# A decode block's output projection: wo in one transfer, all 32 heads projected at once, and more unread matmuls around it

## The chip, the cores and the metric

The kernel runs on one NeuronCore of a Trainium2 chip. The core has a matrix engine (TensorE, PE in the profile; its weight loads are shown apart, as PEld), a vector engine (VectorE, DVE), an activation engine (ScalarE, ACT), GpSimd (POOL) and SyncE (SP), which here only issues DMA transfers. Each engine works through its own list of instructions in order, and they meet through semaphores. The metric is the device time in microseconds (us) of one execution.

## The reference

One token passes a pre-norm transformer block: attention over a cached context, and a gated feed-forward part. Everything is bf16, and the caches are most of the bytes: 32 heads, 4096 positions, 128 values per position, for K and for V.

```python
def _A_ref(x, k_cache, v_cache, wq, wo):          # x [1,1,640]; caches [1,32,4096,128]
    q = (x @ wq).reshape(B, Sq, Hq, Dh).transpose(0, 2, 1, 3)
    scores = einsum("bhqd,bhkd->bhqk", q, k) * Dh ** -0.5
    o = einsum("bhqk,bhkd->bhqd", softmax(scores), v)
    return o.transpose(0, 2, 1, 3).reshape(B, Sq, Hq * Dh) @ wo      # wo [4096, 640]
def _B_ref(x, w_gate, w_up, w_down):              # Df = 1728
    return (gelu(x @ w_gate) * (x @ w_up)) @ w_down
h  = x + _A_ref(layernorm(x), k_cache, v_cache, wq, wo)
h2 = h + _B_ref(layernorm(h), w_gate, w_up, w_down)
```

## The kernel before, in words

**Storage and transfers.** Three large SBUF buffers ("slots") take turns. SyncE issues all the big transfers on one queue, in this order: wq, K0, V0, K1, V1, K2, K3, V2, V3, wo, w_gate, w_up, w_down, where K0 to K3 and V0 to V3 are the caches of eight heads each. A transfer waits until its slot has been read to the end: the third V tile's last reader (`done[("V", 2)]`) frees the slot into which wo goes, and the fourth K tile's last reader frees the one for w_gate. wo comes as two transfers of 2560 KB, one for the rows of heads 0 to 15 and one for those of heads 16 to 31. In each, partition p gets 16 consecutive rows of wo.

**The four groups.** `NG` is 4, and group G has eight heads. For each of eight chunks of a K tile, `score_mult` multiplies K by q on VectorE (L310), eight matmuls against an identity fold the products on TensorE (L318 where the weights are loaded, L30 where they are used again), and `score_sum` reduces them on VectorE (L327). Then `softmax` takes the maximum and the exponentials (L332 to L337) and spreads the weights over a block layout (L341). `attend` multiplies them with V: 64 matmuls (L353). `pick` takes out of their result what belongs to each head (L359, L362, L363), and `head_sum` adds up the partial sums over partitions on TensorE, the softmax denominators with `hb` (L367) and the weighted values with `hs` (L369).

**The pairs of groups.** Two groups make a half of 16 heads, called t. `normalize(t)` divides by the denominators (L373, L374), `spread(t)` copies the 16 rows over all partitions with a matmul against the mask `sel` (L377), and `take(t)` keeps on each partition the values that belong to its rows of wo (L381 with the mask `m8`, then L386, which gives `aP`). `proj_part(t, lo, hi)` then projects: for each i in the range and for each half of wo's 640 columns one matmul of 320 columns, four at a time in different column strips of the array (L398 for the first half of the columns; L30, through `matmul_again`, for the second). The 64 matmuls of both t accumulate in two PSUM banks.

**The order around the change.** It is written out by hand. In the third group (G = 2), while VectorE and TensorE work on the scores, normalize, spread and take of the first half are put between the chunks (after chunks 4, 5 and 6). After the last attend TensorE's list has: eight i of the first half, one unread matmul, the last head sum, four more i, the spread of the second half, the last four i, four unread matmuls, and the 16 i of the second half.

**The unread matmuls.** `run_on(n)` puts n matmuls of 512 columns on TensorE that multiply an identity by itself, into a PSUM bank that nobody reads afterwards. They wait for no other engine. The first is L453 and the others go through `matmul_again`, so that they show as L30 with the names bank<-id_b.

**After the projection.** The sums are copied out of the two banks as a bf16 part and a rest (L469, L470, L471), turned to columns (L477), added to x (L486) and normalized (L487). The gate and up matmuls (L510) wait for w_gate and w_up, the down matmuls (L552, L561) for three parts of w_down, and two copies (L564) lead to the output transfer.

Of the kernel before, what the change touches and what calls it, by code (L numbers as in the profile page):

```python
# [5 lines left out]
FP32 = mybir.dt.float32  # L6
BF16 = mybir.dt.bfloat16
ALU = mybir.AluOpType
ACTF = mybir.ActivationFunctionType
AX = mybir.AxisListType  # L10

D = 640
H = 32
DH = 128
# [6 lines left out]
NG = 4  # L21
# [90 lines left out]
def bass_sequential_preLN__gqa_block_cached__glu_gated_geglu__decode_kernel(nc, A_x, A_k_cache, A_v_cache, A_wq, A_wo, B_x, B_w_gate, B_w_up, B_w_down, out):  # L112
    sb = lambda name, shape, dt: nc.alloc_sbuf_tensor(name, shape, dt)
# [15 lines left out]
    hlnT = sb("hlnT", [128, 5], BF16)  # L129
    rz = sb("rz", [16, 2], FP32)  # L130
    po_r = sb("po_r", [128, 2, DH + 1], FP32)
    m4 = sb("m4", [128, 4], FP32)
    hs = sb("hs", [128, 24], FP32)
    hb = sb("hb", [128, 24], FP32)
    hbx = sb("hbx", [128, 8, 4], BF16)
    aT = sb("aT", [16, 2, 128], BF16)
    aP = sb("aP", [128, 2, 16], BF16)
    sel = sb("sel", [16, 16, 8], BF16)
    m8 = sb("m8", [128, 8], FP32)
    aM = sb("aM", [128, 8, 16], FP32)  # L140
    sel4 = sb("sel4", [128, 4], BF16)
# [20 lines left out]
    class Cut:  # L162
# [3 lines left out]
        def take(self, n, parts=128):  # L166
            ap = self.slot[0:parts, self.at:self.at + n]
            self.at += n
            return ap
    first_t = Cut(slots[2], 5 * 4096)  # L170
    ones_b = first_t.take(128)
    m4_t = first_t.take(128).rearrange("p (a b) -> p a b", a=4)
    hs_t = first_t.take(128).rearrange("p (a b c) -> p a b c", a=8, b=4)
    m8_t = first_t.take(128).rearrange("p (a b) -> p a b", a=8)
    par_t = first_t.take(128).rearrange("p (a b) -> p a b", a=2)
# [18 lines left out]
    wq_sb = slots[2][:, 0:5 * 4096]  # L194
    wo_sb = slots[0][:, 0:32 * D].rearrange("p (t i n) -> p t i n", t=2, i=16)
    wg_sb = slots[2][:, 0:5 * DF].rearrange("p (c n) -> p c n", c=5)
# [39 lines left out]
    def mask(dst, src, pattern, base, cm, op, *deps):  # L236
        return GP(lambda e: e.affine_select(dst, src, pattern=pattern, compare_op=op, fill=0.0, base=base,
                                            channel_multiplier=cm), *deps)
    c_idb = mask(id_b[:, :], ones_b[:, 0:128], [[1, 128]], 0, -1, ALU.is_equal, c_onesb)
    c_hz = GP(lambda e: e.memset(hs[:, :], 0.0))  # L240
    c_bz = GP(lambda e: e.memset(hb[:, :], 0.0))
    c_hb = mask(hb[:, 8:16], ones_b[:, 0:8], [[-16, 8]], 0, 1, ALU.is_ge, c_bz)
    c_hb = mask(hb[:, 8:16], hb[:, 8:16], [[16, 8]], 15, -1, ALU.is_ge, c_hb)
    c_m4 = mask(m4_t, ones_b[:, 0:128].rearrange("p (a b) -> p a b", a=4), [[-1, 4], [-4, 32]], 0, 1, ALU.is_equal)
# [5 lines left out]
    c_hx = mask(hbx[:, :, :], hbx[:, :, :], [[16, 8], [0, 4]], 15, -1, ALU.is_ge, c_hx)  # L250
    c_sel = mask(sel[:, :, :], ones_b[0:16, 0:128].rearrange("p (a b) -> p a b", a=16), [[1, 16], [0, 8]], 0, -1, ALU.is_equal)
    c_m8 = mask(m8_t, ones_b[:, 0:128].rearrange("p (a b) -> p a b", a=8), [[-1, 8], [-8, 16]], 0, 1, ALU.is_equal)

    c_odd = V(lambda e: e.reduce_sum(odd[:, :], hb[:, 8:16].rearrange("p (a b) -> p b a", b=2), axis=AX.X), c_hb)
    c_far = V(lambda e: e.tensor_scalar(far[:, :, :], odd[:, :].unsqueeze(2).to_broadcast([128, 2, 16]), -1e38, 1e38, ALU.mult, ALU.add), c_odd)
    c_m4 = V(lambda e: e.reduce_sum(m4[:, :], m4_t, axis=AX.X), c_m4)
    c_m8 = V(lambda e: e.reduce_sum(m8[:, :], m8_t, axis=AX.X), c_m8)
    c_hs = V(lambda e: e.reduce_sum(hs[:, 8:16], hs_t.rearrange("p a b c -> p a (b c)"), axis=AX.X), c_hs, c_hz)
    c_o4 = V(lambda e: e.reduce_max(ones4[:, :], sel4[:, :], axis=AX.X), c_s4)
# [37 lines left out]
    q1 = V(lambda e: e.tensor_copy(qb[:, :, :].rearrange("p g d -> p (g d)"), ps_q[:, :]), qd)  # L297
    free2 = [qd, c_par, c_m4, c_m8, c_hs, c_idb]

    folds, reds, exps, pbs, pvs, mks, evs, hds, nbs = {}, {}, {}, {}, {}, {}, {}, {}, {}  # L300
    z4s, spr, aPs = {}, {}, {}
    held = [False]

    def other(fn, *d):
        held[0] = False
        return T(fn, *d)
# [58 lines left out]
    def head_sum(G):  # L365
        g, at = G % 2, 132 * (G // 2)
        other(lambda e: e.matmul(ps_a[0:16, at + DH:at + DH + 1], hb[:, 8 - 8 * g:24 - 8 * g], po_r[:, g, DH:DH + 1],  # L367
                                 start=(g == 0), stop=(g == 1), skip_group_check=True), exps[G], z4s.get(G // 2 - 1), c_hb)
        hds[G] = T(lambda e: e.matmul(ps_a[0:16, at:at + DH], hs[:, 8 - 8 * g:24 - 8 * g], po_r[:, g, 0:DH],  # L369
                                      start=False, stop=(g == 1), skip_group_check=True), evs[G], c_hs)  # L370

    def normalize(t):
        rc = V(lambda e: e.reciprocal(rz[:, t:t + 1], ps_a[0:16, 132 * t + DH:132 * t + DH + 1]), hds[2 * t + 1])  # L373
        z4s[t] = V(lambda e: e.tensor_scalar(aT[:, t, :], ps_a[0:16, 132 * t:132 * t + DH], rz[:, t:t + 1], None, ALU.mult), rc)  # L374

    def spread(t):
        spr[t] = other(lambda e: e.matmul(ps_z[:, 32:160], sel[:, :, :].rearrange("p a b -> p (a b)"), aT[:, t, :], start=True, stop=True),  # L377
                       z4s[t], c_sel)

    def take(t):  # L380
        m = V(lambda e: e.tensor_tensor(out=aM[:, :, :], in0=ps_z[:, 32:160].rearrange("p (q i) -> p q i", q=8),  # L381
                                        in1=m8[:, :].unsqueeze(2).to_broadcast([128, 8, 16]), op=ALU.mult), spr[t], c_m8)

        def fn(e):
            with nc.allow_low_precision(reason="one of the eight terms is not zero"):
                return e.reduce_sum(aP[:, t, :], aM[:, :, :].rearrange("p q i -> p i q"), axis=AX.X)  # L386
        aPs[t] = V(fn, m)

    def proj_part(t, lo, hi, *ws):
        def fn(e):  # L390
            for i4 in range(lo, hi, 4):
                for half in range(2):
                    for i in range(i4, i4 + 4):
                        a = 32 * (i - i4)
                        args = (bank[half][a:a + 1, 0:320], aP[:, t, i:i + 1], wo_sb[:, t, i, 320 * half:320 * half + 320])
                        start, stop = t == 0 and i < 4, t == 1 and i >= 12
                        if half == 0:
                            r = e.matmul(*args, start=start, stop=stop)  # L398
                        else:
                            r = matmul_again(nc, *args, start, stop, (128, 32), (0, a))  # L400
            return r
        return T(fn, *ws)

    PARTS = 4
    for G in range(NG):
        for c in range(8):
            if c == 5 and G == 3:
                attend(2)
            score_mult(G, c)
            if c >= 1:  # L410
                score_sum(G, c - 1)
            if c == 1 and G in (1, 2):
                pick(G - 1)
            if c == 3 and G in (1, 2):
                head_sum(G - 1)
            if c == 4 and G == 2:
                normalize(0)
            if c == 5 and G == 2:
                spread(0)
            if c == 6 and G == 2:  # L420
                take(0)
            if c == 7 and G == 3:
                pick(2)
        score_sum(G, 7)
        softmax(G)
        if G == 0:
            load("K", 1, *free2)
            load("V", 1, done[("K", 0)])
        if G == 3:
            head_sum(2)  # L430
        if G != 2:
            attend(G)
        if G == 0:
            load("K", 2, done[("V", 0)])
        if G == 1:
            load("K", 3, done[("K", 1)])
            load("V", 2, done[("V", 1)])
        if G == 2:
            load("V", 3, done[("K", 2)])


    d_wo = [P.dma("sync", wo_sb[:, t, :, :], A_wo[2048 * t:2048 * t + 2048, :].rearrange("(p i) n -> p i n", i=16), done[("V", 2)])
            for t in range(2)]
    free = done[("K", 3)]
# [13 lines left out]
    pick(NG - 1)  # L458
    proj_part(0, 0, 8, aPs[0], d_wo[0], reds[(NG - 1, 7)])
    run_on(1)  # L460
    head_sum(NG - 1)
    normalize(1)
    proj_part(0, 8, 12)
    spread(1)
    take(1)
    proj_part(0, 12, 16)
    run_on(4)
    pr = proj_part(1, 0, 16, aPs[1], d_wo[1])
    hi = [V(lambda e: e.tensor_copy(A_hi[0:97, 0:320], bank[0][0:97, 0:320]), pr),  # L469
# [4 lines left out]
    def columns(part, start):  # L474
# [5 lines left out]
        return fn  # L480
    run_on(1)
    T(columns(A_hi, True), *hi, c_o4)
    run_on(1)
    pr = T(columns(A_lo, False), *lo)
    run_on(1)
    h = V(lambda e: e.tensor_add(hT[:, 0:5], xx[:, 0:5], ps_p[:, 0:5]), pr)  # L486
# [110 lines left out]
```

## Time and profile before

| | |
|---|---|
| time, median of three runs | 201.8 us (201.78 to 201.81) |
| time of the profiled execution | 202.04 us |
| its span, first to last instruction | 200.8 us |
| TensorE, VectorE, ScalarE busy | 112.5, 117.7, 6.5 us |
| bytes read | 84.23 MB, 420 GB/s over the span |
| TensorE's granted clock, mean | 0.907 of full |

The profile is that of one execution. "Busy" times of TensorE are modelled from starts and lengths of pipelined matmuls, so that eight matmuls in a row that each take 0.39 us can follow each other at a much smaller distance. The chain of the profile is the work that ended last, followed back from the last instruction: at each step to what released it, or to the instruction before it on the same engine. In a line such as `L30 x3` the number behind x is the count of instructions, and an arrow `out<-in` names what is written and read. The granted clock is the share of TensorE's full clock that the hardware granted in a stretch.

### The profile page before, as it was taken

To read this page: it belongs to the slowest core of one execution; us is meant where nothing else is said; L and a number is where in the kernel's file an instruction comes from. 1 tells how busy PE (TensorE), PEld (TensorE's weight loads), DVE (VectorE), ACT (ScalarE), POOL (GpSimd) and SP (SyncE) were. 2 spreads that over 40 slices of the span, in tenths; PEclk is the share of its full clock that TensorE was granted. 3 is DMA by queue.
4 is the path that set the end of the run, shared out by engine and by line. 5 is a ranking of instruction groups with operands and counts; after the bars stand their busy time and mean duration, and the time that the engine had idled before them with its cause. 6 is when DMAs were issued, how large, how long until landed. Compare 5 with 4: busy or idle time off the path is not lost.

```text
span 200.8 us, 1539 instructions
## 1 busy us (share of the span) xinstructions
PE 112.5 (56%) x795; PEld 18.2 (9%) x501; DVE 117.7 (59%) x157; ACT 6.5 (3%) x17; POOL 3.5 (2%) x18
## 2 busy tenths in 40 slices
PE   0108000586675808476655095866167697497896
PEld 0103000000001200000021000000000030132423
DVE  3300100889975027999740469898789987814340
ACT  2100000000001000000010000000100000100111
POOL 7000000000000000000000000000000000000000
PEclk9999999999996666999979757899859999879999
DMA  9999999999999999999999999999999999999992
GB/s 343 433 465 431 418 418 418 418 418 496 496 431 444 397 431 418 431 431 418 418 418 421 470 483 444 431 418 431 418 431 431 418 418 388 432 416 435 434 396 97
DMA packets 2316, 84.32 MB, mean 420 GB/s; under 512 B 259, under 2 KB 390, under 8 KB 518
## 3 DMA queue, kind: packets, MB, share of 16 engines
q1 hardware_dynamic: 2308, 84.23, 97.6%
q8 instruction: 5, 0.08, 0.2%
q14 instruction: 1, 0.01, 0.0%
q10 hardware_dynamic: 2, 0.00, 0.0%
HBM read 84.23 MB, written 0.00 MB: 420 GB/s over the span
## 4 chain that ended last, share of the span: by engine, by line
DMA 39%; DVE 33%; PE 25%; ACT 1%; issue 1%; SPq 0%
DMA slot<-in_A_k_cache_dram 39%; DVE slot L310 20%; PE bank L30 11%; PE bank L353 8%; DVE sc L327 6%; PE bank L510 2%; DVE mix L341 1%; PE bank L552 1%; DVE mix L359 1%; PE bank L318 1%; ACT p_t L337 1%; DVE mix L362 1%; DVE mx L332 1%; PE bank L398 0%; DVE slot L471 0%
## 5 line engine op out<-in xcount | busy, mean ns | idle before, releaser
L310 DVE TENSOR_TENSOR slot<-slot,qb 128x4096 bf16<-128x4096 bf16 x32 | 72.7, 2283 | 33.5 <-DMA slot<-in_A_k_cache_dram 33.5
L30 PE MATMUL bank<-slot,id_b 128*128 128x512 bf16 x249 | 66.1, 418 | 27.4 <-DVE slot L310 27.4
L327 DVE TENSOR_REDUCE sc<-bank 128x32 f32<-128x512 f32 x32 | 22.0, 686 | 12.1 <-PE bank L30 12.1
L353 PE MATMUL bank<-slot,mix 128*32 128x512 bf16 x256 | 20.7, 495 | 8.8 <-DVE mix L341 8.8
L318 PE MATMUL bank<-slot,id_b 128*128 128x512 bf16 x7 | 3.4, 484 | 33.5 <-DVE slot L310 33.5
L353 PEld LDWEIGHTS bank<-slot,mix 128*32 128x32 bf16 x256 | 8.0, 120 | 77.6 <-DVE mix L341 42.4
L293 PE MATMUL bank<-slot,xlnM 128*32 128x512 bf16 x40 | 4.5, 630 | 7.2 <-DMA slot<-in_A_wq_dram 7.2
L341 DVE TENSOR_TENSOR mix<-p_t,hbx 128x512 bf16<-128x512 bf16 x16 | 5.7, 420 | 2.7 <-ACT p_t L337 2.7
L337 ACT ACTIVATE p_t<-sc,nb 128x256 bf16<-128x256 f32 x4 | 2.0, 507 | 162.2 <-DVE nb L336 162.2
L297 DVE CAST qb<-bank 128x512 bf16<-128x512 f32 x1 | 0.7, 692 | 10.2 <-PE bank L293 10.2
L359 DVE TENSOR_TENSOR mix<-bank,m 128x512 f32<-128x512 f32 x4 | 2.7, 684 | 4.3 <-PE bank L353 4.3
L266 PE MATMUL bank<-one_bf,x_keep 1*128 1x1 bf16 x5 | 0.4, 177 | 7.0 <-DMA x_keep<-in_A_x_dram 7.0
L453 PE MATMUL bank<-id_b 128*128 128x512 bf16 x11 | 4.2, 384 | 0.0
L318 PEld LDWEIGHTS bank<-slot,id_b 128*128 128x128 bf16 x7 | 0.7, 100 | 36.5 <-DVE slot L310 36.1
L30 PE MATMUL bank<-id_b 128*128 128x512 bf16 x13 | 3.8, 378 | 0.0
L510 PE MATMUL bank<-slot,hlnT 128*1 128x512 bf16 (+1 forms) x40 | 3.6, 478 | 0.1
L367 PEld LDWEIGHTS bank<-po_r,hb 128*16 128x16 f32 x8 | 0.4, 94 | 32.0 <-issue 32.0
L30 PE MATMUL bank<-slot,aP 128*1 128x320 bf16 x32 | 2.5, 298 | 0.0
L398 PE MATMUL bank<-slot,aP 128*1 128x320 bf16 x32 | 2.5, 298 | 0.0
L293 PEld LDWEIGHTS bank<-slot,xlnM 128*32 128x32 bf16 x40 | 1.6, 140 | 9.2 <-issue 9.2
L552 PE MATMUL bank<-slot,hm 128*2 128x160 bf16 x52 | 2.0, 232 | 0.0
L369 PE MATMUL bank<-po_r,hs 128*16 128x128 f32 x8 | 1.5, 274 | 0.6 <-DVE po_r L363 0.6
(94 smaller groups left out, 41.1 us busy)
## 6 DMA issues: line engine op xcount, KB each, us to landing
slot<-in_A_wq_dram SPq DMA_DIRECT2D x1, 5120.0 KB, 15.5
slot<-in_A_wo_dram SPq DMA_DIRECT2D x2, 2560.0 KB, 15.1
slot<-in_B_w_gate_dram SPq DMA_DIRECT2D x1, 2160.0 KB, 16.8
slot<-in_B_w_up_dram SPq DMA_DIRECT2D x1, 2160.0 KB, 21.5
slot<-in_B_w_down_dram SPq DMA_DIRECT2D x1, 1280.0 KB, 24.1
slot<-in_B_w_down_dram SPq DMA_DIRECT2D x1, 640.0 KB, 25.2
slot<-in_B_w_down_dram SPq DMA_DIRECT2D x1, 240.0 KB, 25.3
slot<-in_A_k_cache_dram SPq DMA_DIRECT2D x4, 39.0
```

Of the source, the lines that this page charges most:

```text
L30: return e.add_instruction(mybir.InstMatmult(name=nc.get_next_instruction_name(), engine=e.engine, start_tensor_calc=start, stop_tensor_ca ...
L293: i = e.matmul(ps_q[32 * j:32 * j + 32, :], xlnM[:, 160 * s + 32 * c:160 * s + 32 * c + 32], wq_j[:, c, 2 * j + s, :, :], start=(c == 0 an ...
L310: m = V(lambda e: e.tensor_tensor(out=kt, in0=kt, in1=qb[:, G, :].unsqueeze(1).to_broadcast([128, 32, DH]), op=ALU.mult), landed[("K", G)] ...
L318: i = e.matmul(*args, start=True, stop=False)
L327: reds[(G, c)] = V(lambda e: e.reduce_sum(sc[:, 32 * c:32 * c + 32], ps_f[c % 2][:, :].rearrange("p (g d) -> p g d", d=16), axis=AX.X), fo ...
L337: exps[G] = A(lambda e: e.activation(p_t[:, :], sc[:, :], ACTF.Exp, bias=nb[:, G:G + 1], scale=INV_SQRT_DH, accum_out=po_r[:, G % 2, DH:DH ...
L341: pbs[(G, n)] = pbs[G] = V(lambda e, lo=lo, hi=hi: e.tensor_tensor(out=p_bd[:, lo:hi, :].rearrange("p c (a r) -> p c a r", a=8), in0=p_t[: ...
L353: i = e.matmul(po[a:a + 32, 0:512], p_bd[:, c, :], vt[:, 4 * c:4 * c + 4, :], start=(c < 4), stop=(c >= 60))
L359: mks[G] = V(lambda e: e.tensor_tensor(out=po_m, in0=po[:, 0:512].rearrange("p (b d) -> p b d", b=4), in1=m4[:, :].unsqueeze(2).to_broadca ...
L453: i = e.matmul(*args, start=True, stop=True)
L510: i = e.matmul(po[32 * a:32 * a + 1, 512 * k:512 * k + 128 * n], hlnT[:, c:c + 1], cols, start=(c == 0), stop=(c == 4))
L552: i = e.matmul(ps_d[32 * t:32 * t + 2, :], hm[:, at:at + 2], wd_sb[:, PIECE * c + 160 * t:PIECE * c + 160 * t + 160], start=False, stop=(c ...
```

## The change

wo comes in one transfer of 5120 KB, in which partition p gets 32 consecutive rows. The four groups' head sums go to 32 partitions of one PSUM region, and normalize, spread and take are done once, for all 32 heads, after the last head sum; they leave the third group. Correspondingly `rz`, `aT`, `aP`, `sel` and `aM` are laid out for 32 heads, the mask `m8` with eight columns is gone and `m4` with four takes its place in `take`, and `hs` and `hb` grow from 24 to 56 columns. The projection is one block of 64 matmuls behind `take`.

The unread matmuls are set anew: three between the last attend and the last head sum, one between normalize and spread, twelve between take and the projection, then 2, 3 and 2 where there were 1, 1 and 1 in the steps behind the projection. Counted out of the diff, there are 16 up to the projection's end where there were 5, and 7 behind it where there were 3.

```diff
-    rz = sb("rz", [16, 2], FP32)
+    rz = sb("rz", [32, 1], FP32)
...
-    aT = sb("aT", [16, 2, 128], BF16)
-    aP = sb("aP", [128, 2, 16], BF16)
-    sel = sb("sel", [16, 16, 8], BF16)
-    m8 = sb("m8", [128, 8], FP32)
-    aM = sb("aM", [128, 8, 16], FP32)
+    aT = sb("aT", [32, 128], BF16)
+    aP = sb("aP", [128, 32], BF16)
+    sel = sb("sel", [32, 32, 4], BF16)
+    aM = sb("aM", [128, 4, 32], FP32)
...
-    wo_sb = slots[0][:, 0:32 * D].rearrange("p (t i n) -> p t i n", t=2, i=16)
+    wo_sb = slots[0][:, 0:32 * D].rearrange("p (i n) -> p i n", i=32)
...
     def head_sum(G):
-        g, at = G % 2, 132 * (G // 2)
-        other(lambda e: e.matmul(ps_a[0:16, at + DH:at + DH + 1], hb[:, 8 - 8 * g:24 - 8 * g], po_r[:, g, DH:DH + 1],
-                                 start=(g == 0), stop=(g == 1), skip_group_check=True), exps[G], z4s.get(G // 2 - 1), c_hb)
-        hds[G] = T(lambda e: e.matmul(ps_a[0:16, at:at + DH], hs[:, 8 - 8 * g:24 - 8 * g], po_r[:, g, 0:DH],
-                                      start=False, stop=(g == 1), skip_group_check=True), evs[G], c_hs)
...
+        lo = 24 - 8 * G
+        other(lambda e: e.matmul(ps_a[0:32, DH:DH + 1], hb[:, lo:lo + 32], po_r[:, G % 2, DH:DH + 1],
+                                 start=(G == 0), stop=(G == 3), skip_group_check=True), exps[G], c_hb)
+        hds[G] = T(lambda e: e.matmul(ps_a[0:32, 0:DH], hs[:, lo:lo + 32], po_r[:, G % 2, 0:DH],
+                                      start=False, stop=(G == 3), skip_group_check=True), evs[G], c_hs)
+
+    def normalize():
+        rc = V(lambda e: e.reciprocal(rz[:, :], ps_a[0:32, DH:DH + 1]), hds[3])
+        return V(lambda e: e.tensor_scalar(aT[:, :], ps_a[0:32, 0:DH], rz[:, 0:1], None, ALU.mult), rc)
+
+    def spread(z):
+        return T(lambda e: e.matmul(ps_z[:, 32:160], sel[:, :, :].rearrange("p a b -> p (a b)"), aT[:, :], start=True, stop=True), z, c_sel)
+
+    def take(sp):
+        m = V(lambda e: e.tensor_tensor(out=aM[:, :, :], in0=ps_z[:, 32:160].rearrange("p (q i) -> p q i", q=4),
+                                        in1=m4[:, :].unsqueeze(2).to_broadcast([128, 4, 32]), op=ALU.mult), sp, c_m4)
...
+                return e.reduce_sum(aP[:, :], aM[:, :, :].rearrange("p q i -> p i q"), axis=AX.X)
+        return V(fn, m)
+
+    def proj(e):
+        for i4 in range(0, 32, 4):
+            for half in range(2):
+                for i in range(i4, i4 + 4):
+                    a = 32 * (i - i4)
+                    args = (bank[half][a:a + 1, 0:320], aP[:, i:i + 1], wo_sb[:, i, 320 * half:320 * half + 320])
+                    if half == 0:
+                        r = e.matmul(*args, start=(i < 4), stop=(i >= 28))
+                    else:
+                        r = matmul_again(nc, *args, i < 4, i >= 28, (128, 32), (0, a))
+        return r
...
-            if c == 4 and G == 2:
-                normalize(0)
-            if c == 5 and G == 2:
-                spread(0)
-            if c == 6 and G == 2:
-                take(0)
...
-    d_wo = [P.dma("sync", wo_sb[:, t, :, :], A_wo[2048 * t:2048 * t + 2048, :].rearrange("(p i) n -> p i n", i=16), done[("V", 2)])
-            for t in range(2)]
+    d_wo = P.dma("sync", slots[0][:, 0:32 * D], A_wo[:, :].rearrange("(p i) n -> p (i n)", i=32), done[("V", 2)])
...
     pick(NG - 1)
-    proj_part(0, 0, 8, aPs[0], d_wo[0], reds[(NG - 1, 7)])
+    run_on(3)
+    head_sum(NG - 1)
+    z = normalize()
     run_on(1)
-    head_sum(NG - 1)
-    normalize(1)
-    proj_part(0, 8, 12)
-    spread(1)
-    take(1)
-    proj_part(0, 12, 16)
-    run_on(4)
-    pr = proj_part(1, 0, 16, aPs[1], d_wo[1])
+    sp = spread(z)
+    pw = take(sp)
+    run_on(12)
+    pr = T(proj, pw, d_wo, reds[(NG - 1, 7)])
...
-    run_on(1)
+    run_on(2)
     T(columns(A_hi, True), *hi, c_o4)
-    run_on(1)
+    run_on(3)
     pr = T(columns(A_lo, False), *lo)
-    run_on(1)
+    run_on(2)
```

## The prediction, made before the result was known

> **What bounds the kernel now.** I read the page's chain by line first, then the chain in order of time from 172 us on, then the timeline around the edited lines, the landings of wo, the waits of the last loads, and the windows with the granted clock. The page says that transfers and VectorE hold the chain:
>
> ```profile
> span 200.8 us, 1539 instructions
> DMA 39%; DVE 33%; PE 25%; ACT 1%; issue 1%; SPq 0%
> ```
>
> The transfer part ends at 113.06 us, when the third K tile lands. From there to the end the chain has compute only. Its end, in order of time (start, length, what):
>
> ```profile
> 174.69 5.22 PE bank L353 x63
> 179.94 0.70 DVE mix L359
> 182.10 0.35 DVE aT L374
> 182.50 0.23 PE bank L377
> 183.09 0.32 PE bank L453
> 183.41 0.65 PE bank L30 x3
> 184.06 0.24 PE bank L398 x4
> 185.29 0.50 DVE slot L469
> 192.64 1.08 PE bank L30 x5
> 193.72 1.76 PE bank L510 x14
> ```
>
> The reader is to see that TensorE runs in program order through L377 (spread), four unread matmuls (L453 and L30) and the second half of the projection, and that L30 x5, unread matmuls again, run right up to the up-projection at 193.72. So there is no free time between the projection and the end: what delays L469 delays the last copy.
>
> The first half of the heads: part of the work that the change removes, in the timeline:
>
> ```profile
> 129.72 0.68 DVE L327 TENSOR_REDUCE sc<-bank 128x32 f32<-128x512 f32 x1
> 130.33 0.14 DVE L373 RECIPROCAL rz<-bank 16x1 f32<-16x1 f32 x1
> 130.51 0.34 DVE L374 TENSOR_SCALAR aT<-bank,rz 16x128 bf16<-16x128 f32 x1
> 130.77 2.27 DVE L310 TENSOR_TENSOR slot<-slot,qb 128x4096 bf16<-128x4096 bf16 x1
> 132.97 0.67 DVE L327 TENSOR_REDUCE sc<-bank 128x32 f32<-128x512 f32 x1
> ```
>
> And the windows (start:end and length; busy time with instructions of PE, PEld, DVE, ACT, POOL; then the granted clock, the DMA share and GB/s):
>
> ```profile
> 167.65:171.06 3.41, 2.16 (x11) 0.00 (x0) 3.38 (x4) 0.00 (x0) 0.00 (x0) 1.00 0.80 339
> 171.06:174.48 3.42, 1.04 (x7) 0.22 (x4) 2.58 (x8) 0.60 (x2) 0.00 (x0) 1.00 0.98 419
> 174.48:177.89 3.41, 3.19 (x32) 1.25 (x36) 1.17 (x4) 0.00 (x0) 0.00 (x0) 0.50 1.00 426
> 177.89:181.30 3.41, 2.99 (x55) 1.11 (x39) 1.29 (x3) 0.00 (x0) 0.00 (x0) 1.00 0.99 422
> 181.30:184.72 3.42, 2.89 (x47) 0.80 (x28) 1.28 (x5) 0.00 (x0) 0.00 (x0) 1.00 0.99 423
> ```
>
> A window in which TensorE was busy for 1.04 of 3.42 us is followed by one at half clock; one with 2.16 is not. In the same view 119.86:123.28, with 1.36 busy, is also followed by half clock. From 177.89 to the last matmul the clock is full.
>
> **The change part by part.** The profiled execution took 202.04 us, its span 200.8 and 1.24 around it; the median of the three runs, 201.8, is 0.24 less. The sum is made on the trace and its difference put on the median. All shifts below are against the trace's own times.
>
> *Removed from VectorE in the third group (L373, L374, L381, L386 for the first 16 heads).* From the start of L327 to that of the next L310 normally takes 0.60 us (132.97 to 133.57). With normalize it takes 1.05 (129.72 to 130.77), with take 1.19 (135.77 to 136.96). So 0.45 + 0.59 = 1.04 us go. VectorE is the bound there: TensorE's folds of 1.89 us wait for L310 each time. Every later idle of VectorE up to 174 us is a wait for a TensorE fold that itself follows L310, so it moves along. The transfers needed are early: the last V tile is issued at 141.21 and takes 29.9 us to land, at 171.1, and the matmuls that read it start at 174.69. Bounds: nothing gained (a rival below), and 1.12, the sum of the four busy times; I take 1.04, the difference of starts. The removed L377 of that stage (0.23) sat in TensorE's idle time and is worth nothing.
>
> *Through the last attend (L353).* It starts at 173.65 instead of 174.69. The window 171.06 to 174.48 then holds 0.83 us of it and some 0.1 of the head sum, less than the 1.04 before, so 174.48 to 177.89 stays at half clock. At full clock its 64 matmuls take 3.57 us by the earlier one at 161.34, 0.054 each; at half clock 0.107. That is 15 matmuls by 174.48, 32 more by 177.89, and 17 x 0.054 = 0.92 us after it: L359 starts at 179.02, not 179.94. Of the 1.04 us, 0.92 arrive.
>
> *Removed from here: 16 matmuls of the projection, one unread matmul; added: three unread.* They stand between attend and the last head sum while VectorE runs L359 to L363 (1.5 us, ending at 180.50). Three at 0.217 (0.65 for three in the chain) end near 179.7. No cost; without that cover it would be 0.65. Losing the first projection half here and its other 16 matmuls below is paid for further down.
>
> *Head sum, reciprocal, normalize and spread with 32 rows or columns instead of 16.* No row shows them at 32. L369 takes 0.28 at 16 columns, and L273, fp32 with 128 columns, 0.27; L374 is 0.34 on 16 partitions, and L363 on 128 partitions with 128 fp32 elements 0.29. I take the old values, with -0.05 and +0.2 as ends. Spread then starts at 182.50 - 0.92 = 181.58. Take reads the same 128 elements (0.29 + 0.37), ends near 182.5 and is covered by what follows; were it doubled, still.
>
> *Twelve unread matmuls behind spread, where there were 8 of the projection and four unread.* They wait for nothing, and the projection is queued behind them on TensorE. They start at 181.78 (182.50 to 182.65 from L377 to the next start, and up to 0.1 for the larger weight load, half of it taken), 12 x 0.217 = 2.60 us, then the 0.1 seen between the last unread matmul and L398: the projection starts at 184.48 instead of 183.99. Without the twelve it could start when wo has landed. Ends: 0.214 each (eight folds in 1.89, less the 0.39 of one, over seven), and 0.427 at half clock (3.42 for the eight folds at 147.47), which is a rival below.
>
> *The whole projection at once.* In the timeline each group of four matmuls starts 0.136 us after the last (183.99 to 184.94 for seven steps). Sixteen groups instead of eight are 8 x 0.136 = 1.09 us more on the path. L469 starts at 185.29 + 0.49 + 1.09 = 186.87: 1.58 later.
>
> *Unread matmuls after it: 2, 3 and 2 for 1, 1 and 1.* In all the edit has 23 for 8 before. Two fit under L469 (0.50), three (0.65) end about when L471 ends, two end before L273. I take 0.05; ends 0 and 0.4.
>
> *wo in one transfer.* The second half is issued at 165.3 and lands 18.0 us later:
>
> ```profile
> DMA to landing us min/median/max: 12.2/15.1/18.0
> ```
>
> That is 183.3, behind the last V tile on a queue that is full (0.99 and 1.00 share above). One load of the same bytes lands there too, whenever it is issued; 0.3 us to either side. At 184.48 it is hidden. SP saves one issue of 0.43 ahead of w_gate, which waits for the last fold anyway. The masks of the setup are built in POOL's 3.5 us before wq lands at 15.6; nothing.
>
> Sum: -0.92 upstream, +1.41 until the projection's start, +1.09 for its second half, +0.05: **+1.63 on the trace, so 201.8 + 1.6 = 203.4 us.** With all the small ends low it is 203.2, high 204.0.
>
> *A rule against the trace's price.* The Trainium skill, "TensorE: Matmul & The Clock Gate", section "Back-to-back issue gap", puts a sustained stream of load-and-matmul pairs at 131 ns for 512 columns. By that figure twelve are an estimated 1.57 us, the projection starts near 183.45 and the time is 202.4. The chain's three at 0.65 say 0.217 each, and the unread ones reuse one weight, so I give it 2 in 100.
>
> **The rivals.**
>
> *Upstream gain lost.* If the 1.04 us go into a half-clock window instead (146 to 151 us, where folds run at 0.427), all 0.92 are missing: 204.3. Against it: all of that stage's first fold is at half clock before and after; of the second 0.73 us would now be, so that it ends at 152.1, and VectorE reads it at 152.7 after the next L310. 8 in 100.
>
> *The last attend at full clock.* If its windows fall otherwise, so that none has little TensorE work, attend takes 3.57 from 173.65 and L359 starts at 177.3. Then the twelve end at 182.8, and wo's landing at 183.3 is what is late next: the projection starts 0.6 earlier than before, its second half still adds 1.09, so 202.3. For it: the share between 1.36 and 2.16 that decides. Against: three runs within 0.03 us. 15 in 100. The Trainium skill, same page, section "What's actually happening", says the window is free-running and does not reset when a kernel starts. By that this case would be likelier than I make it; the agreement of the runs speaks against such a spread, but no row here shows two phases.
>
> *The clock falls in the tail.* If 177.89 to 181.30 drops to under 1.4 us of TensorE work, half the clock falls on the twelve: about seven run by 184.72, five after it, and the projection starts near 185.9: 204.8. I count 2.6 us of work there: attend 1.1, three unread 0.7, head sum 0.6, one unread 0.2. 7 in 100.
>
> *Not slower: the last transfers set the end.* The waits name them:
>
> ```profile
> PEld bank L510 <- DMA slot<-in_B_w_up_dram: 1.3, 1, 1.3
> ```
>
> If TensorE were really ready for L510 1.6 us before w_up lands, the delay would vanish there and the time stay at 201.8. It decides from 1.6 us of slack. w_up is issued at 172.0 and lands 21.5 later, 193.5; but the unread matmuls in front end at 193.72, so the slack is nothing. 5 in 100.
>
> **How the numbers follow.** My forecast has 60 in 100; the rivals 8, 15, 7, 5 and the rule's 2; 3 are left for what I don't see, 2 of them faster. The time is that of the forecast, 203.4. The range 202.2 to 204.4 takes in the full-clock attend below and the lost gain above, and leaves out the tail's clock, the hidden delay and the unseen. Faster or slower by over 0.2% (0.4 us, about what a measurement of this kernel tells from none): the full-clock case sits at that edge, a third of it counts as the same. With the hidden delay that gives same 0.10, faster 0.02, slower 0.88.
>
> **What would show it.** In the changed kernel's trace: L327 to L310 near 0.60 throughout the third group; the last attend a microsecond earlier and half its clock gone until the same moment; twelve unread matmuls at 0.217 between spread and the projection, with the aP reduction long done; wo landed before the projection; sixteen groups at 0.136; and w_up and w_down landed well before L510 and L552 start. Wrong would be a projection that starts at wo's landing, a half-clock window after 178 us, or a wait of L510 or L552 on a transfer.

## The result, and the profile after

Over 22 executions each, the changed kernel has a median of 202.32 us (201.99 to 203.72), the kernel before 201.81 (201.73 to 202.15). The ratio is 1.003, with a 95% interval of 1.0018 to 1.0042: slower by 0.5 us, where I had forecast 1.6. The changed kernel's times lie in two heaps: most between 202.0 and 202.8, four from 203.3 to 203.72. The profiled execution is one of the long four, at 203.36; the other three left no trace.

The head of its page, and the page's chain by engine:

```profile
span 202.1 us, 1547 instructions
DMA 38%; DVE 32%; PE 26%; ACT 1%; issue 1%; SPq 0%
```

The end of its chain in order of time (start, length, what). Line numbers have moved: L348 is attend, L372 spread, L437 and L30 the unread matmuls, L390 the projection, L451 the copy behind it, L492 the gate and up matmuls:

```profile
173.54 5.35 PE bank L348 x64
178.92 0.70 DVE mix L354
181.08 0.35 DVE aT L369
181.48 0.23 PE bank L372
181.71 0.32 PE bank L437
182.03 2.37 PE bank L30 x11
184.40 0.24 PE bank L390 x4
186.72 0.50 DVE slot L451
194.05 1.08 PE bank L30 x5
195.13 1.76 PE bank L492 x14
```

This execution went as the prediction had it: attend 1.15 us earlier than before (I had said 1.04), spread at 181.48 (181.58), the twelve before the projection and its first matmul at 184.33 in the timeline (184.48), the copy at 186.72 (186.87). Against the profiled execution of before it is 1.32 us longer. So the puzzle is not this execution. It is that most others are about 1.1 us shorter, and that the kernel before has no such spread in these 22 executions. (In the later sets below a few of its executions reach 202.47 and 202.6.)

### The profile page after: what moved, and what is told of

Read it like the earlier page. It is cut to its first block, busy times and chain, and to the rows that moved or that the text cites. A ratio compares the mean times of both kernels' runs of the same rounds, so it can differ in the third digit from the quotient of the medians.

```text
span 202.1 us, 1547 instructions
## 1 busy us (share of the span) xinstructions
PE 117.3 (58%) x809; PEld 18.4 (9%) x500; DVE 116.5 (58%) x152; ACT 6.5 (3%) x17; POOL 3.4 (2%) x17
## 4 chain that ended last, share of the span: by engine, by line
DMA 38%; DVE 32%; PE 26%; ACT 1%; issue 1%; SPq 0%
DMA slot<-in_A_k_cache_dram 38%; DVE slot L305 20%; PE bank L30 13%; PE bank L348 8%; DVE sc L322 6%; PE bank L492 2%; DVE mix L336 1%; DVE mix L354 1%; PE bank L534 1%; PE bank L313 1%; ACT p_t L332 1%; DVE mix L357 1%; DVE mx L327 1%; PE bank L437 1%; PE bank L390 1%
## 5 line engine op out<-in xcount | busy, mean ns | idle before, releaser
L305 DVE TENSOR_TENSOR slot<-slot,qb 128x4096 bf16<-128x4096 bf16 x32 | 72.7, 2281 | 33.2 <-DMA slot<-in_A_k_cache_dram 33.2
L30 PE MATMUL bank<-slot,id_b 128*128 128x512 bf16 x250 | 68.3, 427 | 25.8 <-DVE slot L305 25.8
L322 DVE TENSOR_REDUCE sc<-bank 128x32 f32<-128x512 f32 x32 | 21.9, 684 | 12.6 <-PE bank L30 12.6
L348 PE MATMUL bank<-slot,mix 128*32 128x512 bf16 x256 | 20.5, 491 | 8.7 <-DVE mix L336 8.7
L313 PE MATMUL bank<-slot,id_b 128*128 128x512 bf16 x6 | 3.0, 498 | 32.8 <-DVE slot L305 32.8
L348 PEld LDWEIGHTS bank<-slot,mix 128*32 128x32 bf16 x256 | 8.0, 119 | 82.5 <-DVE mix L336 42.1
L30 PE MATMUL bank<-id_b 128*128 128x512 bf16 x27 | 7.4, 378 | 0.0
L437 PE MATMUL bank<-id_b 128*128 128x512 bf16 x12 | 4.6, 384 | 0.0
L492 PE MATMUL bank<-slot,hlnT 128*1 128x512 bf16 (+1 forms) x40 | 3.6, 477 | 0.1
L362 PEld LDWEIGHTS bank<-po_r,hb 128*32 128x32 f32 x8 | 0.5, 108 | 32.7 <-issue 32.7
L451 DVE CAST slot<-bank 97x320 bf16<-97x320 f32 x1 | 0.5, 492 | 4.3 <-PE bank L30 4.3
L30 PE MATMUL bank<-slot,aP 128*1 128x320 bf16 x32 | 2.2, 299 | 0.0
L390 PE MATMUL bank<-slot,aP 128*1 128x320 bf16 x32 | 2.2, 299 | 0.0
```

Source lines behind the costliest of these rows:

```text
L30: return e.add_instruction(mybir.InstMatmult(name=nc.get_next_instruction_name(), engine=e.engine, start_tensor_calc=start, stop_tensor_ca ...
L305: m = V(lambda e: e.tensor_tensor(out=kt, in0=kt, in1=qb[:, G, :].unsqueeze(1).to_broadcast([128, 32, DH]), op=ALU.mult), landed[("K", G)] ...
L313: i = e.matmul(*args, start=True, stop=False)
L322: reds[(G, c)] = V(lambda e: e.reduce_sum(sc[:, 32 * c:32 * c + 32], ps_f[c % 2][:, :].rearrange("p (g d) -> p g d", d=16), axis=AX.X), fo ...
L348: i = e.matmul(po[a:a + 32, 0:512], p_bd[:, c, :], vt[:, 4 * c:4 * c + 4, :], start=(c < 4), stop=(c >= 60))
L390: r = e.matmul(*args, start=(i < 4), stop=(i >= 28))
```

## The experiments

My first theory, A, was that executions differ by where the half-clock windows fall, on the last attend above all. Rivals: B, the transfers vary; C, the clock varies earlier, in the third group's first folds; D, a floor behind the projection takes up part of any delay.

**Another execution of each kernel.** The changed kernel again, with no edit:

> The changed kernel as it is, for another execution's trace. Theory A (the clock's windows fall differently from execution to execution): where the last attend (L348, 64 matmuls) runs at full clock it takes about 3.6 us, the twelve unread matmuls are over by 183.0 and the projection starts at wo's landing near 183.1 instead of 184.33, for a time near 202.1; where it runs at half clock it takes 5.3 us and the time is near 203.3. Most executions are of the first kind. Rival B (the transfers vary): attend takes 5.3 us in every execution, and wo and w_down land later in the longer ones.

Eleven executions had a median of 202.43 us (201.93 to 203.49). The traced one, at 202.06, belongs to the short heap, and yet its attend takes 5.20 us, at half clock. Theory A had the wrong place. The difference is the third group's second fold. The chain of the long execution, then of this one (L305 is the multiplication, L322 the sum, L30 the fold):

```profile
120.84 2.21 DVE slot L305
123.10 3.51 PE bank L30 x8
126.63 0.69 DVE sc L322
```

```profile
120.81 2.20 DVE slot L305
123.01 0.60 DVE sc L322
123.61 2.20 DVE slot L305
```

In the long one VectorE waits for a fold of 3.51 us, in the short one it does not wait at all. The windows say why, first the long execution, then the short one (the clock stands behind the five engines):

```profile
119.56:122.97 3.41, 1.37 (x7) 0.00 (x0) 3.34 (x5) 0.00 (x0) 0.00 (x0) 1.00 1.24 538
122.97:126.38 3.41, 3.28 (x8) 0.00 (x0) 2.87 (x3) 0.00 (x0) 0.00 (x0) 0.50 0.80 346
```

```profile
120.96:124.37 3.41, 1.95 (x10) 0.00 (x0) 3.41 (x3) 0.00 (x0) 0.00 (x0) 1.00 0.89 384
124.37:127.78 3.41, 2.50 (x14) 0.10 (x4) 3.41 (x3) 0.00 (x0) 0.00 (x0) 1.00 1.15 500
```

The same work is cut differently: a window with 1.37 us of TensorE work is followed by half clock, one with 1.95 is not. Both executions began the group at 112.8. That settles C for these two; the K tile's transfer did not differ, so not B. Behind this fold the short execution is 0.9 us ahead, from 150 us on 1.1, because the fourth group's first fold at half clock takes 3.38 us in it and 3.59 in the long one, and behind the last attend 1.27. Its projection starts at 183.06, right behind the twelve unread matmuls; wo had landed just before, near 182.9 (issued at 162.68, 20.2 us to landing).

The kernel before again, with no edit:

> The kernel before as it is, for another execution's trace. If the execution shown before was one of the longer ones (202.04 against a median of 201.8), a usual one has the second fold of the third group (near 123 us) at full clock, reaches the projection's second half at wo's landing near 183.2 instead of 183.99, and starts the up matmuls (L510) when w_up lands, near 193.4, instead of behind the unread matmuls at 193.72: time 201.75. If the chain is free of transfers in all executions, as my prediction had it, L510 again follows the unread matmuls directly.

One execution, 201.98 us, with the mechanism as expected; its chain from 113 us on shows no waiting for the second fold either. Its timeline:

```profile
183.09 0.31 PE L398 MATMUL bank<-slot,aP 128*1 128x320 bf16 x4 [1.15 <-DMA slot<-in_A_wo_dram]
184.38 0.49 DVE L469 CAST slot<-bank 97x320 bf16<-97x320 f32 x1 [3.06 <-PE bank L30]
193.53 1.80 PE L510 MATMUL bank<-slot,hlnT 128*1 128x512 bf16 x20 [0.73 <-DMA slot<-in_B_w_up_dram]
```

The projection's second half waits 1.15 us for wo, and the up matmuls, idle for 0.73 us, wait for w_up. In the execution of before that I had read TensorE stood idle for neither. That this one is still at 201.98 is w_up's doing: L510 starts at 193.53, where executions traced further down get w_up at 193.2 and end at 201.7. So rival B has a part too, of some 0.3 us. The same three moments in the changed kernel's short execution, from its chain (matmuls behind unread ones are counted there from the end of those; in the timeline the projection starts at 183.06 and the up matmuls at 193.78):

```profile
183.13 0.24 PE bank L390 x4
185.45 0.50 DVE slot L451
193.85 1.74 PE bank L492 x14
```

The projection starts at the same moment in both. It ends 1.07 us later, which is the 8 x 0.136 of the half that was hidden before. At the up matmuls 0.25 us are left of that (193.78 against 193.53), because 0.73 are taken from the wait for w_up, and in the time 0.08 (202.06 against 201.98).

This pair differs by less than the medians do. What sets the time of an execution can be read across all traces, those of the experiments below included. Where the up matmuls wait for w_up in one piece, the time is 8.44 to 8.45 us behind their start (201.98 for 193.53, and 201.64, 201.68 and 201.72 for 193.19, 193.24 and 193.27). Where they don't wait, and the clock holds behind the projection, it is 18.05 us behind the start of the projection's second half in the kernel before (202.04 for 183.99, 202.27 for 184.21), and 19.0 behind the start of the whole projection in the changed one (202.06 for 183.06, 202.34 for 183.29, 202.54 for 183.53, 203.36 for 184.33). So in the execution of before at 201.98, with its second half at 183.09, the wait for w_up hid an estimated 0.84 us (183.09 + 18.05 is 201.14). By the same sums the changed kernel's median of 202.32 stands for a projection that starts near 183.3. Whether the twelve or wo's landing sets that start in the median execution is not shown: the only two traces of the unedited changed kernel start behind the twelve.

**Attend at full clock** (the definition of `run_on` moves up for this and is not shown).

```diff
         if G == 3:
             head_sum(2)
+            run_on(11)
```

> The changed kernel with eleven more unread matmuls between the third head sum and the last attend, in 2.6 us in which TensorE is idle, so that no window before attend is nearly empty. Theory A: every execution has attend at full clock (3.6 us), the projection starts at wo's landing, the median stays near 202.1 and nothing is left near 203.3. Rival B: the spread from 202.0 to 203.7 stays, with the median near 202.3. Rival C (the spread comes from the first folds of the third group, 113 to 127 us, at half clock): the spread stays too, though attend takes 3.6 us in each.

Measured 202.20 us (202.12 to 202.54), and nothing near 203.3. In the trace the projection waits 1.96 us for wo:

```profile
183.53 0.31 PE L390 MATMUL bank<-slot,aP 128*1 128x320 bf16 x4 [1.96 <-DMA slot<-in_A_wo_dram]
```

This agrees with A in its numbers, and not with what I had expected under C, that the spread stays. But it doesn't prove A's place: attend's gain of 1.7 us would cover a slow fold in the third group too. What it shows is the floor, wo's landing and then 64 matmuls. The same edit to the kernel before:

> The kernel before with eleven more unread matmuls between the third head sum and the last attend. If its longer executions (202.0 to 202.5) are those whose last attend, or a fold of the third group before it, ran at half clock, attend now takes 3.6 us in all of them, wo's landing and then w_up's are waited for in all, and the times lie within 201.65 and 201.95, median 201.75. If the longer ones come from the transfers, the upper ones stay.

Measured 201.88 (201.64 to 202.91), beside 201.92 for before: the median is near the 201.75 that I had expected, but two long executions (202.32 and 202.91) stayed, against what I had expected. The traced one waits 0.3 us for w_up and is not a long one. What made the others long was not traced; the last experiment below shows a cause that fits.

**Half of the projection** (the `stop` conditions move from 28 to 12 with it; half of the heads are then left out of the result).

```diff
-        for i4 in range(0, 32, 4):
+        for i4 in range(0, 16, 4):
```

> The changed kernel with only the first 16 of the 32 steps of the projection (32 matmuls of 64, so that half of the heads' contribution is left out of the result). In the traces a step of four matmuls is 0.136 us, eight of them 1.09. My prediction's price (all of it on the path): 202.3 - 1.1 = 201.2. Theory D (behind the projection stands a floor that the last transfers set, near 201.75): the median falls only to 201.75, by 0.3 to 0.5, and L492's second half (up) waits for w_up.

Measured 201.81 us (201.63 to 202.37), ratio to before 1.000 (0.9991 to 1.0008). With 1.09 us of the projection gone the time falls by 0.5 (0.6 against the set at 202.43, measured together with it), not by 1.1. Theory D holds; the chain of the traced execution names the floor:

```profile
169.96 23.24 DMA slot<-in_B_w_up_dram
193.24 1.85 PE bank L492 x14
```

**The twelve unread matmuls.** Without them:

```diff
     pw = take(sp)
-    run_on(12)
     pr = T(proj, pw, d_wo, reds[(NG - 1, 7)])
```

> The changed kernel without the twelve unread matmuls between spread and the projection. Theory A: an execution with attend at half clock starts its projection at wo's landing or at the end of the aP reduction, whichever is later, near 183.1, 1.2 us earlier than 184.33, so the longest times fall from 203.3 to 202.1; the others, which wait for wo already, keep 202.1; median 202.1, spread under 0.4. If instead the unread matmuls hold the clock up at the end (the reason against taking them away), the projection runs at half clock and the time is 203 or more.

> The changed kernel without the twelve unread matmuls, once more. Theory E (they hold the clock): TensorE does little between the last attend and wo's landing, a half-clock window falls on the projection, its groups of four take 0.27 us instead of 0.136, and the time is near 204.1. Theory A: the projection starts at wo's landing at full clock, 202.1 to 202.3.

Three executions of the first gave 203.87 to 204.24; a fourth is told of in the last section. The second gave 203.52 (202.12 to 204.45) over six executions, ratio 1.0069 (1.0036 to 1.0103). Theory A, which had put it at 202.1 to 202.3, fell here too. The windows of the traced execution, at 203.64, and its chain:

```profile
179.31:182.72 3.41, 0.83 (x4) 0.20 (x3) 1.15 (x4) 0.00 (x0) 0.00 (x0) 1.00 0.94 405
182.72:186.13 3.41, 2.96 (x48) 0.88 (x28) 0.00 (x0) 0.00 (x0) 0.00 (x0) 0.50 1.03 441
```

```profile
162.54 20.49 DMA slot<-in_A_wo_dram
183.17 0.44 PE bank L390 x3
183.60 0.27 PE bank L30 x4
183.87 0.27 PE bank L390 x4
```

TensorE has 0.83 us of work in the window before wo's landing, the clock is halved in the next, and the projection's groups of four take 0.27 us instead of 0.136. So the unread matmuls earn their place. With four of them:

> The changed kernel with four unread matmuls instead of twelve before the projection. Where the twelve end late (184.33 in the longer executions) eight fewer bring the projection forward to wo's landing near 183.1, so nothing above 202.6 is left, if the clock holds; the median 202.2. Theory E: with 0.87 us of unread work instead of 2.6 the window before the projection comes near the share that decides, some executions get half clock in the projection and take about 204, and the median is worse than 202.4.

Measured 202.32 us (201.97 to 204.62), ratio 1.0061 (1.0029 to 1.0092): seven executions up to 202.34, five from 203.8 on. The two heaps are as theory E had them; its median, worse than 202.4, was not met. The traced one, a short one, has 1.81 us of TensorE work in the window before wo's landing and keeps the clock. Twelve in the kernel before, in place of its four:

```diff
-    run_on(4)
+    run_on(12)
     pr = proj_part(1, 0, 16, aPs[1], d_wo[1])
```

> The kernel before with twelve unread matmuls instead of four ahead of the projection's second half; nothing else is changed. In a usual execution (spread at 180.4) they end near 183.5, 0.4 us after wo's landing, and the 0.73 us that L510 waits for w_up take that up: median 201.8 to 201.9, no change. In the longer ones (spread at 182.5) they end at 185.6, 1.7 us later than the four, nothing takes that up, and the time is near 203.7. My prediction's price (all of it on the path in every execution) would put the median at 203.5.

Measured 202.46 us (201.78 to 203.46), ratio 1.0027 (1.001 to 1.0044). The price, 0.5 us, is between my two figures. Spread came at 180.99 in the trace, 0.6 us later than the 180.4 that I had reckoned with; eight matmuls of the projection and then the twelve followed, and the second half started at 184.21, 1.1 us behind wo's usual landing instead of 0.4. The longest executions, two at 203.46, are near the 203.7 that I had named for those with a late spread, but were not traced. So twelve unread matmuls alone cost the kernel before as much as the whole change does.

**wo in two transfers, four unread matmuls, the rest of the change kept.**

```diff
-    d_wo = P.dma("sync", slots[0][:, 0:32 * D], A_wo[:, :].rearrange("(p i) n -> p (i n)", i=32), done[("V", 2)])
+    d_wo = [P.dma("sync", wo_sb[:, 16 * t:16 * t + 16, :], A_wo[:, :].rearrange("(p i) n -> p i n", i=32)[:, 16 * t:16 * t + 16, :],
+                  done[("V", 2)]) for t in range(2)]
...
-    run_on(12)
-    pr = T(proj, pw, d_wo, reds[(NG - 1, 7)])
+    run_on(4)
+    T(lambda e: proj(e, 0, 16), pw, d_wo[0], reds[(NG - 1, 7)])
+    pr = T(lambda e: proj(e, 16, 32), d_wo[1])
```

> The changed kernel with wo in two transfers again (steps 0 to 15 in the first, 16 to 31 in the second), four unread matmuls, and the first 32 matmuls of the projection waiting for the first transfer alone. They start when aP is ready, near 181.3 to 182.5, and the second 32 at the second landing, 183.1, or later, so the projection ends at 184.3 to 184.9 instead of 185.4: back to the floor that w_up and w_down set, median 201.75 to 201.9, like before. If the half projection hidden beside the last attend before was what mattered, rather than the wait for the whole wo, it stays at 202.2 or more.

Measured 201.88 us (201.65 to 202.00), ratio 0.9997 (0.9988 to 1.0006): the whole loss is gone, and no execution is long. In the timeline the first half of the projection starts behind aP, the second behind the second landing:

```profile
181.66 0.23 PEld L390 LDWEIGHTS bank<-slot,aP 128*1 128x1 bf16 x8 [0.87 <-DVE aP L380]
183.00 0.23 PEld L390 LDWEIGHTS bank<-slot,aP 128*1 128x1 bf16 x8 [0.57 <-DMA slot<-in_A_wo_dram]
```

The run above with four unread matmuls differs from this one only in that wo comes in one piece (202.32, and five of twelve executions from 203.8 on). So merging the heads costs nothing that can be seen here; making the first 32 matmuls wait for all of wo does. Twelve unread matmuls with wo in two pieces were not run. The end is w_up's again:

```profile
169.91 23.32 DMA slot<-in_B_w_up_dram
193.27 1.85 PE bank L494 x14
```

**Can the floor be lowered?** The kernel before, with w_up cut in two:

```diff
-    d_wu = P.dma("sync", wu_sb, B_w_up[:, :].rearrange("(p c) n -> p c n", c=5))
+    wu_v = B_w_up[:, :].rearrange("(p c) n -> p c n", c=5)
+    d_wu = [P.dma("sync", wu_sb[:, a:b, :], wu_v[:, a:b, :]) for a, b in ((0, 3), (3, 5))]
...
-    run_on(6, ps_s[:, :])
-    up = T(glu(1, 5 * DF, range(5)), d_wu, c_po)
+    run_on(2, ps_s[:, :])
+    T(glu(1, 5 * DF, range(3)), d_wu[0], c_po)
+    up = T(glu(1, 5 * DF, range(3, 5)), d_wu[1])
```

> The kernel before with w_up in two transfers (three of its five parts, then two), the up matmuls of the first three parts issued ahead of the wait for the rest, and two unread matmuls instead of six ahead of them. If w_up's landing sets the end, 12 of the 20 up matmuls are done by then, up ends near 194.3 instead of 195.3, and the end moves to w_down's third landing near 198.4: 201.5 to 201.6. If w_down's landings set the end already, nothing changes (201.75); if the four unread matmuls held the clock, it is 202 or more.

Measured 202.04 us (201.84 to 202.17), ratio 1.0000 (0.9992 to 1.0009): nothing changes, and the clock stays full from the projection on. The up matmuls still wait 0.33 us for w_up, the down matmuls now wait 0.58 and 0.29 for the parts of w_down, and the end stayed:

```profile
171.86 26.27 DMA slot<-in_B_w_down_dram
198.17 0.92 PE bank L554 x20
```

With the eleven unread matmuls as well:

> Both edits to the kernel before at once: w_up in two transfers and eleven unread matmuls ahead of the last attend. Expected 201.5 to 201.6, and all executions within 0.2 us of each other, because the clock cannot fall before the last attend and the last transfer sets the end in each.

Measured 201.95 us (201.79 to 202.75), ratio 1.0003 (0.9992 to 1.0013). Wrong in the time and in the spread: the traced execution is a long one, at 202.72, and its windows show the price of coming early.

```profile
180.19:183.61 3.42, 1.50 (x24) 0.31 (x9) 0.48 (x2) 0.00 (x0) 0.00 (x0) 1.00 0.97 406
183.61:187.02 3.41, 3.23 (x41) 0.99 (x21) 1.38 (x3) 0.42 (x1) 0.00 (x0) 0.50 0.99 425
```

Attend ended early, TensorE stood idle 1.92 us for wo, and the clock was half from 183.61 to 193.85. For the kernel before with the eleven alone this is the likeliest cause of its long executions, argued and not shown. No version beat the kernel before, the one with half a projection included.

## Why the prediction was wrong, point by point

*"There is no free time between the projection and the end."* This step failed. It was true of the execution that I read. In the other execution of before, the up matmuls stand idle for 0.73 us until w_up lands. The rival that the last transfers set the end, which I dismissed with a slack of "nothing" and 5 in 100, holds for that part; it takes 0.73 of the 1.09 us at the up matmuls, and an estimated 0.84 at the end. What the experiments show in place of the step is a floor: with half the projection gone the time stops at 201.81, where the up matmuls start as w_up lands (193.24).

*The sum put on the median.* I saw that the profiled execution was 0.24 us above the median and treated that as an offset. It was another course of the clock: its second fold of the third group ran at half clock (123.28 to 126.69 in my own windows). In such an execution the kernel before loses some 0.2 to 0.3 us (202.04 against a median of 201.81; all 22 times lay between 201.73 and 202.15), because it then uses up the waits for wo and w_up; the changed kernel, which has little left of them, loses 1.3 (203.36 against 202.06). My sum of 1.63 was for a pair of such executions, and that pair measures 1.32. In the changed kernel the times near it are the minority, four of 22. The sign was in the rows that I had read: w_up landed at 193.5 there, 0.2 us before the up matmuls started behind the unread ones. An execution 0.24 us shorter, such as the median one, should by this already wait for that landing (worked out from these rows; the shorter executions of before in that set left no trace).

*+1.41 until the projection's start, less the upstream gain.* In the shown execution 184.33 against 183.99, +0.34 where I had +0.49. In the traces of the two other executions it is nothing: 183.09 in the kernel before, held by wo's landing, and 183.06 in the changed one, where the twelve end just behind that landing. There the upstream gain and the twelve cancel. The 1.04 us were real up to the end of the third group (143.90 against 145.21, of which 0.27 came from an earlier start of the group); the next fold, at half clock, took 0.17 longer, so that attend came 1.15 earlier. The twelve fill the time up to wo's landing.

*+1.09 for the projection at once.* Right: sixteen groups at 0.136, 1.07 later at the copy behind it.

*The unread matmuls behind the projection, and the 32-row forms.* Right: from the copy to the gate matmuls 4.17 us before and 4.16 after; from the last head sum to spread 1.02 before and 1.03 after; from spread to the projection 2.85, where I had 2.90.

*The rival with attend at full clock, 202.3.* Its number is what was measured, and its cap (wo's landing is what is late next) is what the runs show. Its place was wrong: the one short execution of the changed kernel that was traced has attend at half clock, and gains its time in the third group. That the number fits is owed to the cap, which holds wherever the time is gained, and so in part to luck. Three runs within 0.03 us were my evidence against a varying clock course. They were no evidence, because the kernel before hides most of what the course of the clock does. What I cited from the Trainium skill, "TensorE: Matmul & The Clock Gate", section "What's actually happening", that the window is free-running, agrees with the traces: the edges lie at 119.56 and 122.97 in one execution of the changed kernel, and at 120.96 and 124.37 in another.

*The twelve as pure cost.* Wrong in kind. Without them, and with wo in one piece, the median is 203.52.

*The Trainium skill's 131 ns for 512 columns.* Not seen: eleven take 2.37 us in the chain, 0.215 each. They reuse one weight, so this is not the stream of load-and-matmul pairs that the figure is for.

## What to carry to other kernels

A profile is one execution. Where the granted clock changes in windows that can fall anywhere, check in a second trace which waits appear when the chain is a microsecond earlier, before calling a chain free of slack. Splitting a large load lets the part of the work that needs only its first half run in time that would be spent waiting for the second; here 1.09 us of matmuls, of which the median saw about half. In these runs unread matmuls before a wait cost nothing until they outlasted it, and taking them away cost more than they took.

## What the runs showed of the hardware that I had not expected

The amount of TensorE work after which the clock falls is not sharp in this profile's busy times: a window with 1.45 of 3.41 us kept the full clock in the changed kernel with eleven more unread matmuls, and one with 1.50 lost it in the last experiment. Those times are modelled, so the rule itself may well be sharp.

The way back was not the same everywhere either. In the execution of before that I read, one window at half clock with 3.19 of 3.41 us of TensorE work was followed by full clock; in the last experiment's, windows with 3.23 and 3.41 were followed by half clock again. Why is open.

One execution without the twelve took 560.47 us. On its page the folds' matmuls take 1705 ns in the mean, 427 in the changed kernel, while VectorE's multiplications take 2282 ns, as ever, and the granted clock of its profile is 1.00. It is left out above, and its cause is open.
